# Inputs of the third and fourth superblock turned by VectorE and transfers through DRAM in place of TensorE

## The chip, the core and the metric

The kernel runs on one core of a Trainium2 chip. A core has engines with a queue of instructions each, worked off in order: TensorE (PE; matmuls, and the loading of their stationary operand, PEld), VectorE (DVE), ScalarE (ACT), GpSimd (POOL), and SyncE (SP), which here only issues transfers (DMAs). They meet at semaphores. Sixteen DMA engines move data between DRAM and the on-chip memory SBUF, whose 128 partitions are the first axis of every tile. TensorE writes to PSUM, a smaller memory of eight banks. The metric is the device time of one execution in microseconds (us).

## The reference

One transformer block with modulated normalization. `x` is 2048 rows of 512; `F` is 1376; all is 32-bit.

```python
mod = (silu(c) @ w_mod).reshape(1, 6, 1, 512)          # sa, ca, ga, sb, cb, gb
h = layernorm(x) * (1 + ca) + sa
x = x + ga * irfft2(rfft2(h) * (w_r + 1j * w_i))       # over rows and columns
h = layernorm(x) * (1 + cb) + sb
a = mish(h @ w1 + b1)                                  # 512 -> 1376
x = x + gb * (a @ w2)                                  # 1376 -> 512
```

## The kernel before

The first part (to about 90 us) does the spectral filter; its last phase, `p3_col` and `p3_row`, brings each of the 16 row tiles of `x` (128 rows each, kept in SBUF as `x[:, n, :]`) up to date. Then comes the second half, the two dense layers, which are interleaved with that last phase.

The two layers work on 8 blocks `b` of 256 rows, that is of two row tiles; two blocks are a superblock `i` (0 to 3, four row tiles `4i` to `4i + 3`). The hidden axis has six tiles `t`: five of 256 columns, and a single one, `t = 0`, of 96. Every 32-bit product is made of three terms: an operand is split into a high part, rounded by a ScalarE cast, and the rest, a VectorE subtraction (`split`, L848 to L850). Most tiles use a Strassen-like scheme with seven block products in place of eight. The right operands of the first layer are eight slots per superblock, four blocks of the transposed input (`B11`, `B12`, `B21`, `B22`) and four sums of them (`T1` to `T4`).

The steps on the way of an input are these.

- `norm_one(n)` (L207): ScalarE writes the normalized row tile `n` to a buffer of tag `h`, of which there are two.
- `next_in` (for the first superblock `first_in`) has two parts. `transpose_in` (L768) turns four pieces of 128x128 by TensorE into one PSUM bank of tag `D`; `scale_in` (L776) has ScalarE scale and shift them, two instructions of 128x256, into a buffer of tag `t` or `y`. Each superblock has four such steps, so 16 transposes.
- `sum_in` (L787) and `split_in` (L793, L794) make the eight slots.
- `up` (L914; `up_single`, L963, for the tile of 96) is one block product of the first layer, six matmuls into PSUM; its weights come from a ring of eight buffers `wr`, filled from DRAM by `fetch_w1` on SP's queue (L722), which waits there until the buffer is free. `evict` and `mish_odd` apply bias and activation. `sums` and `halves` (L987, L849, L850) prepare the activations, and `down` (L1017; L1013 for the tile of 96; `last_down` at the end, L1029 and L1032) is a piece of the second layer, three matmuls.
- `gather`, `chain` and `residual` bring a block's results together; a GpSimd DMA adds them to `x` in place (L1069), and `store` writes two row tiles of `x` to the output (L1078, SP's queue). After `store` the row tiles of that block are not read again. `load_last` later loads second-layer weights into `x[:, 0:2]`, `x[:, 2:4]`, `x[:, 4:6]` and `x[:, 6]` and multiplies them by the gate (L869).

The order of all this is written out by hand. `plan.at(key, fn, ...)` enters each step with a key; the steps are sorted by key and numbered, and the list `ORDER` then gives the sequence in which the numbers are issued. This sequence is the program order of every engine's queue. Below, "step 442" is the place in that sequence, counted from 0. A step's instructions go to the queues of their engines; between engines only data dependencies hold.

Of the kernel before, what the change touches and what calls it, by code (L numbers as in the profile page):

```python
# [7 lines left out]
F32 = mybir.dt.float32  # L8
F32R = mybir.dt.float32r
AF = mybir.ActivationFunctionType  # L10
ALU = mybir.AluOpType

P = 128
# [18 lines left out]
POOL_LOW = range(1, 15, 2)  # L32

ORDER = (
# [43 lines left out]
)  # L78


# [1 line left out]
def tile_spectral_block(ctx: ExitStack, tc: tile.TileContext, x_d, w1_d, b1_d, w2_d,  # L82
                        c_d, xt_d, wm_d, wq_d, wz_d, kr_d, km_d, kc_d, ki_d, kf_d, kv_d, kw_d, kp_d, out_d):
    nc = tc.nc
# [8 lines left out]
    dram = ctx.enter_context(tc.tile_pool(name="dram", bufs=1, space=bass.MemoryType.DRAM))  # L93
# [20 lines left out]
    def buf(tag, dt=F32):  # L114
        return work.tile([P, 512], dt, name="buf", tag=tag)

    def plain(t):
        return t.bitcast(F32)

    x = base.tile([P, N2, D], F32, name="x")  # L120
# [9 lines left out]
    cols = base.tile([P, 2, 2, 4], F32, name="cols")  # L130
# [82 lines left out]
    st = {}  # L213
# [483 lines left out]
    odd = [pm.tile([P, 512], F32, name=f"odd{i}") for i in range(4)]  # L697
    slots = {b: pm.tile([P, 2, 2, 256], F32R, name=f"h{b}") for b in ("B11", "B21")}
    wsum = pm.tile([P, 512], F32, name="wsum")
    ring, raws, src, temps, stage = {}, {}, {}, {}, {}  # L700

    def flat2(t):
        return t.rearrange("p a b -> p (a b)")
# [67 lines left out]
    def scale_in(b, g, dst):  # L771
        raws[b] = dst
        ps = st.pop("pt2")
        for e in range(2):
            k = 2 * g + e
            nc.scalar.activation(dst[:, 256 * e:256 * e + 256], ps[:, 256 * e:256 * e + 256],  # L776
                                 AF.Identity, bias=cols[:, 1, 0, k:k + 1], scale=cols[:, 1, 1, k:k + 1])

    def part(b, i):
        return slots[b][:, i].rearrange("p k s -> p (k s)")  # L780

# [4 lines left out]
        raws[b] = raws[dst] if dst in raws else dst if dst is not None else buf("h")  # L786
        nc.vector.tensor_tensor(raws[b], p, q, op=op)  # L787

    def split_in(b):
        r = raws[b]  # L790
        if b not in slots:
            slots[b] = pm.tile([P, 2, 2, 256], F32R, name="h" + b, tag="h" + b)
        nc.scalar.copy(part(b, 0), r)  # L793
        nc.vector.tensor_tensor(part(b, 1), r, plain(part(b, 0)), op=ALU.subtract)  # L794

    def p3_col(n):
        d = dd[n // 8][:, n % 8]
# [307 lines left out]
    plan = Plan()  # L1105
# [90 lines left out]
    for k, (i, t, j) in enumerate(units):  # L1196
# [6 lines left out]
        if (i, t) in PLAIN:  # L1203
            f, e = int(j[0][1]) - 1, int(j[1][2]) - 1
# [11 lines left out]
    for b in range(NB):  # L1216
        for t in DOWN if b < NB - 1 else (1, 2, 3, 4, 5, 0):
# [14 lines left out]
            n = len(order(b, t))  # L1232
# [14 lines left out]

    for i in range(1, NB // 2):
        u = where[i, 1, 1] - 39
        for n, s in ((0, 14.5), (1, 15.5), (2, 19.5), (3, 20.5)):  # L1250
            plan.at(u + s, norm_one, 4 * i + n)
        for b, n, g, s in (("B11", 0, 0, 17), ("B21", 0, 1, 18), ("B12", 2, 0, 23), ("B22", 2, 1, 25)):
            plan.at(u + s + 0.3, next_in, b, 4 * i + n, g)
        split_at, sum_at = (((35.2, 36.2, 37.2, 38, 37.5, 38.7, 40, 40.5), (35.4, 38.2, 36.5, 39.2)) if i == 1 else
                            ((33.3, 33.8, 37.3, 38.3, 39.3, 40.3, 41.3, 42.3), (34.65, 35.15, 36.65, 38.15)))
        for b, s in zip(("B11", "B12", "B21", "T2", "T1", "T3", "T4", "B22"), split_at):
            plan.at(u + s, split_in, b)
        for (b, dst), s in zip((("T1", "B11"), ("T3", "B12"), ("T2", None), ("T4", "B21")), sum_at):
            plan.at(u + s, sum_in, b, dst)

# [184 lines left out]
```

## Time and profile before

| | |
|---|---|
| median of 3 runs | 375.84 us (375.76 to 377.65) |
| profiled execution, its own time | 375.52 us |
| its span, first to last instruction | 373.7 us |
| TensorE clock granted | 0.997 |
| TensorE busy | 366.8 us |
| VectorE busy | 304.8 us |
| ScalarE busy | 252.5 us |
| DMA | 81.59 MB, 218 GB/s mean |

In rows of groups, the columns are: line, engine, operation, output and inputs, shapes, count, then the busy time in us and the mean ns of one, then the engine's idle time ahead of them and what ended it. The busy time of overlapping instructions is counted once, so for pipelined matmuls it is less than count times mean. In rows of the timeline the first number is the start in us from the span's start, the second how long the merged piece lasted. In rows of DMA issues the last number is the median time from issue to landing.

### The profile page before, as it was taken

To read this page: it belongs to the slowest core of one execution; us is meant where nothing else is said; L and a number is where in the kernel's file an instruction comes from. 1 tells how busy PE (TensorE), PEld (TensorE's weight loads), DVE (VectorE), ACT (ScalarE), POOL (GpSimd) and SP (SyncE) were. 2 spreads that over 40 slices of the span, in tenths; PEclk is the share of its full clock that TensorE was granted. 3 is DMA by queue.
4 is the path that set the end of the run, shared out by engine and by line. 5 is a ranking of instruction groups with operands and counts; after the bars stand their busy time and mean duration, and the time that the engine had idled before them with its cause. 6 is when DMAs were issued, how large, how long until landed. Compare 5 with 4: busy or idle time off the path is not lost.

```text
span 373.7 us, 8193 instructions
## 1 busy us (share of the span) xinstructions
PE 366.8 (98%) x2916; PEld 351.8 (94%) x2916; DVE 304.8 (82%) x752; ACT 252.5 (68%) x553; POOL 65.0 (17%) x102
## 2 busy tenths in 40 slices
PE   8999999998999999999999999999999999999995
PEld 8999967777999999999999999999999999999994
DVE  2898968888989989999994589884569895788996
ACT  1798879996557869999666865665865653365750
POOL 0588738784000000000000100000000000000000
PEclk9999999999999999999999999999999999999998
DMA  7999998777734545677874696747855858695132
GB/s 244 366 323 352 344 375 302 227 211 262 240 132 148 202 142 184 220 256 242 290 232 151 181 233 214 209 140 192 261 147 194 209 185 283 158 332 137 45 58 112
DMA packets 44359, 81.59 MB, mean 218 GB/s; under 512 B 6784, under 2 KB 12000, under 8 KB 44064
## 3 DMA queue, kind: packets, MB, share of 16 engines
q1 hardware_dynamic: 41152, 70.46, 56.8%
q0 software_dynamic: 1008, 3.67, 6.0%
q10 hardware_dynamic: 2160, 6.95, 5.8%
q8 instruction: 23, 0.38, 0.4%
q14 instruction: 16, 0.13, 0.1%
HBM read 64.02 MB, written 13.37 MB: 207 GB/s over the span
## 4 chain that ended last, share of the span: by engine, by line
PE 91%; DVE 6%; issue 1%; ACT 0%; DVEq 0%; ACTq 0%
PE bank L914 28%; PE bank L1017 24%; PE bank L802 4%; PE bank L812 4%; PE bank L803 4%; PE bank L547 4%; PE bank L257 4%; PE bank L963 3%; PE bank L596 3%; PE bank L302 3%; PE bank L1013 3%; PE bank L527 2%; PE bank L768 2%; PE bank L313 1%; PE bank L304 1%; PE bank L303 1%
## 5 line engine op out<-in xcount | busy, mean ns | idle before, releaser
L1069 POOL DMA_DIRECT2D x<-modr x7 | 6.2, 889 | 263.6 <-ACT buf L776 121.4
L914 PE MATMUL bank<-hT,wr 128*128 128x256 f32 x360 | 51.2, 283 | 0.0
L914 PEld LDWEIGHTS bank<-hT,wr 128*128 128x128 f32 x360 | 46.7, 191 | 0.1
L914 PE MATMUL bank<-hB,wr 128*128 128x256 f32 x300 | 43.5, 284 | 0.0
L914 PEld LDWEIGHTS bank<-hB,wr 128*128 128x128 f32 x300 | 39.1, 191 | 0.0
L850 DVE TENSOR_TENSOR al<-buf,ah 128x512 fp32r<-128x512 f32 (+1 forms) x45 | 29.9, 668 | 7.9 <-ACT ah L849 7.6
L1017 PE MATMUL bank<-w2a,ah 128*128 128x256 f32 x161 | 35.1, 283 | 0.0
L1017 PE MATMUL bank<-w2b,ah 128*128 128x256 f32 x147 | 32.3, 283 | 0.0
L849 ACT CAST ah<-buf 128x512 fp32r<-128x512 f32 (+1 forms) x45 | 26.8, 604 | 7.0 <-PE bank L1017 5.8
L914 PE MATMUL bank<-hcr,wr 128*128 128x256 f32 x210 | 30.3, 284 | 0.0
L914 PEld LDWEIGHTS bank<-hcr,wr 128*128 128x128 f32 x210 | 27.3, 191 | 0.0
L1017 PEld LDWEIGHTS bank<-w2a,ah 128*128 128x128 f32 x161 | 26.8, 191 | 0.0
L802 PE MATMUL bank<-kc,d 128*128 128x128 f32 x128 | 24.8, 276 | 0.5 <-ACT d L440 0.5
L803 PE MATMUL bank<-kc,d 128*128 128x128 f32 x128 | 24.8, 275 | 0.0
L1017 PEld LDWEIGHTS bank<-w2b,ah 128*128 128x128 f32 x147 | 24.7, 192 | 0.0
L171 DVE BATCH_NORM_STATS2 st<-x 128x6 f32<-128x512 f32 x32 | 21.9, 686 | 0.2 <-DMA x<-in_A_x_dram 0.2
L1017 PE MATMUL bank<-w,ah 128*128 128x256 f32 x112 | 21.7, 286 | 0.0
L302 PE MATMUL bank<-buf,mring 128*128 128x512 f32 x48 | 20.6, 430 | 0.2 <-DVE buf L295 0.2
L802 PEld LDWEIGHTS bank<-kc,d 128*128 128x128 f32 x128 | 19.4, 192 | 0.7 <-ACT d L440 0.7
L803 PEld LDWEIGHTS bank<-kc,d 128*128 128x128 f32 x128 | 19.4, 192 | 0.0
L805 ACT COPY buf<-bank 128x512 f32<-128x512 f32 x16 | 9.4, 584 | 14.8 <-PE bank L803 14.6
L776 ACT ACTIVATE buf<-bank,cols 128x256 f32<-128x256 f32 x28 | 14.2, 565 | 6.7 <-PE bank L768 6.5
(292 smaller groups left out, 1102.8 us busy)
## 6 DMA issues: line engine op xcount, KB each, us to landing
wr<-w_S SPq DMA_DIRECT2D x60, 256.0 KB, 3.1
wr<-w_A SPq DMA_DIRECT2D x45, 256.0 KB, 3.1
w_S<-hT SPq DMA_DIRECT2D x20, 256.0 KB, 2.4
x<-in_A_x_dram SPq DMA_DIRECT2D x16, 256.0 KB, 4.9
xring<-in_x_t_dram SPq DMA_DIRECT2D x16, 256.0 KB, 5.1
w_A<-wr SPq DMA_DIRECT2D x15, 256.0 KB, 4.4
x<-modr POOLq DMA_DIRECT2D x7, 512.0 KB, 5.7
out_dram<-x SPq DMA_DIRECT2D x7, 512.0 KB, 4.5
```

Source lines behind the costliest of these rows:

```text
L171: nc.vector.bn_stats(t, x[:, n, :])
L257: nc.tensor.matmul(pgv[:, j], data(j), krs[:, j, :].rearrange("p (c q) -> p c q", c=2), start=True, stop=True)
L302: nc.tensor.matmul(pa, m[:, a, 0:128], g, start=(i == 0), stop=False)
L547: nc.tensor.matmul(pb[:, 0:w], kf[:, 0:128], z[:, 0:w], start=True, stop=True)
L776: nc.scalar.activation(dst[:, 256 * e:256 * e + 256], ps[:, 256 * e:256 * e + 256], AF.Identity, bias=cols[:, 1, 0, k:k + 1], scale=cols[: ...
L802: nc.tensor.matmul(o, dj[:, 0:128], kc[0][:, n, :], start=True, stop=False)
L803: nc.tensor.matmul(o, dj[:, 64:192], kc[1][:, n, :], start=False, stop=True)
L812: nc.tensor.matmul(px[:, j * P:(j + 1) * P], e[:, j * P:(j + 1) * P], kiv[:, j, :], start=True, stop=True)
L849: nc.scalar.copy(h, r)
L850: nc.vector.tensor_tensor(l, r, plain(h), op=ALU.subtract)
L914: nc.tensor.matmul(o, w[:, p, k, :], h[:, q, k, :], start=(first and n == 0), stop=(last and n == 5), skip_group_check=True)
L1017: nc.tensor.matmul(out_ps[b][n][:, 256 * half:256 * half + 256], a[p][:, e], w2[t][q][:, r], start=(t == 1 and half == 0 and i == 0), stop ...
```

## The change

For the third and fourth superblock (`i` of 2 and 3) `next_in` is replaced. The normalized row tile (`norm_one` as before) is turned by VectorE in square blocks of 32x32 (`turn_one`), two row tiles interleaved into a pair of row tiles of `x` that has been stored: rows 0 and 1 of `x` for both pairs of the third superblock, rows 2 and 3 and then 0 and 1 for those of the fourth. Four DMAs per pair, each from 32 partitions, write it to a DRAM tile so that the blocks come to their place (`turn_out`, 128 KB each, pieces of 1 KB). One DMA per slot reads 128 partitions of four pieces of 512 bytes back (`turn_in`, 256 KB). ScalarE then scales and shifts in place in SBUF (`scale_turned`, two instructions of 128x256 elements as before). The elements of a slot lie in another order than before, so `split_in` reads them through a rearranged view for these superblocks. The keys of these steps differ, and `ORDER` is another list, with 1170 numbers in place of 1150: all steps, also those the change doesn't otherwise touch, are dealt out anew.

```diff
 ORDER = (
-    "3 1 0 14 4 2 16 21 15 5 7 6 52 8 10 123 73 12 71 17 11 13 26 118 75 19 38 32 9 44 125 24 47 80 22-23 33 18 82 "
...
+    "3 1 0 2 5 16 21 52 6 15 7 32 8 10 4 12 17 13 11 14 73 24 19 38 47 26 9 22 75 62 23 71 27 20 69 118 18 25 29 "
...
+    def turning(row):
+        return x[:, row:row + 2, :].rearrange("p r d -> p (r d)").rearrange("p (c k n j) -> p c k n j", c=4, k=4, n=2)
+
+    def turn_one(n, row):
+        nc.vector.transpose(turning(row)[:, :, :, n % 2],
+                            st.pop(("h2", n)).rearrange("p (k c j) -> p c k j", k=4, c=4))
+
+    def turn_out(n, row):
+        turned[n] = t = dram.tile([P, 4, 256], F32, name=f"turned{n}")
+        for a in range(4):
+            nc.sync.dma_start(t[:, a].rearrange("(c i) s -> i c s", c=4),
+                              x[32 * a:32 * a + 32, row:row + 2, :].rearrange("i r d -> i (r d)")
+                              .rearrange("i (c s) -> i c s", c=4))
+
+    def turn_in(b, n, g):
+        raws[b] = dst = buf("ty"["B12 B22".find(b) >= 0])
+        nc.sync.dma_start(dst.rearrange("p (a s) -> p a s", a=4), turned[n][:, :, 128 * g:128 * g + 128])
+
+    def scale_turned(b, g):
+        for e in range(2):
+            k, o = 2 * g + e, raws[b].rearrange("p (a k s) -> p k a s", a=4, k=2)[:, e]
+            nc.scalar.activation(o, o, AF.Identity, bias=cols[:, 1, 0, k:k + 1], scale=cols[:, 1, 1, k:k + 1])
...
-    def split_in(b):
+    def split_in(b, i=0):
         r = raws[b]
...
-        nc.scalar.copy(part(b, 0), r)
-        nc.vector.tensor_tensor(part(b, 1), r, plain(part(b, 0)), op=ALU.subtract)
+        h, l = part(b, 0), part(b, 1)
+        if i > 1:
+            r = r.rearrange("p (a m j) -> p m a j", a=4, m=4)
+            h, l = (z.rearrange("p (m a j) -> p m a j", a=4, m=4) for z in (h, l))
+        nc.scalar.copy(h, r)
+        nc.vector.tensor_tensor(l, r, plain(h), op=ALU.subtract)
...
     for i in range(1, NB // 2):
         u = where[i, 1, 1] - 39
-        for n, s in ((0, 14.5), (1, 15.5), (2, 19.5), (3, 20.5)):
-            plan.at(u + s, norm_one, 4 * i + n)
-        for b, n, g, s in (("B11", 0, 0, 17), ("B21", 0, 1, 18), ("B12", 2, 0, 23), ("B22", 2, 1, 25)):
-            plan.at(u + s + 0.3, next_in, b, 4 * i + n, g)
+        if i == 1:
+            for n, s in ((0, 14.5), (1, 15.5), (2, 19.5), (3, 20.5)):
+                plan.at(u + s, norm_one, 4 * i + n)
+            for b, n, g, s in (("B11", 0, 0, 17), ("B21", 0, 1, 18), ("B12", 2, 0, 23), ("B22", 2, 1, 25)):
+                plan.at(u + s + 0.3, next_in, b, 4 * i + n, g)
+        else:
+            for n, row, s in ((0, 2 * i - 4, 19.5), (1, 2 * i - 3, 20.5), (2, 0, 22.5), (3, 1, 23.5)):
+                plan.at(u + s, norm_one, 4 * i + n)
+                plan.at(u + s + 0.3, turn_one, 4 * i + n, row - n % 2)
+                if n % 2:
+                    plan.at(u + s + 0.4, turn_out, 4 * i + n - 1, row - 1)
+            for b, n, g, s in (("B11", 0, 0, 25), ("B21", 0, 1, 25.5), ("B12", 2, 0, 28), ("B22", 2, 1, 28.5)):
+                plan.at(u + s, turn_in, b, 4 * i + n, g)
+                plan.at(u + s + 2, scale_turned, b, g)
...
         for b, s in zip(("B11", "B12", "B21", "T2", "T1", "T3", "T4", "B22"), split_at):
-            plan.at(u + s, split_in, b)
+            plan.at(u + s, split_in, b, i)
```

More of the change, by code (lines that the diff above doesn't have):

```diff
@@ L699, in tile_spectral_block @@
     wsum = pm.tile([P, 512], F32, name="wsum")
-    ring, raws, src, temps, stage = {}, {}, {}, {}, {}
+    ring, raws, src, temps, stage, turned = {}, {}, {}, {}, {}, {}
     def flat2(t):
```

85 rows, old and new, of the table ORDER are left out of this document.

## The prediction

> **What bounds the kernel now.** I read the page's first part, then the stretches of 10 us, then TensorE's timeline around the transposes, the groups, and last the DMA issues and the waits of SP's queue.
>
> ```profile
> span 373.7 us, 8193 instructions
> PE 366.8 (98%) x2916; PEld 351.8 (94%) x2916; DVE 304.8 (82%) x752; ACT 252.5 (68%) x553; POOL 65.0 (17%) x102
> PE 91%; DVE 6%; issue 1%; ACT 0%; DVEq 0%; ACTq 0%
> ```
>
> The profiled execution took 375.52 us (span 373.7 and 1.8 around it); the median of the runs is 375.84, so 0.3 is added at the end. TensorE holds 91% of the chain. Whether it is merely busy or truly without gaps is told by the stretches (columns: PE, PEld, DVE, ACT, POOL busy us of 10, clock, DMA share, GB/s):
>
> ```profile
> 200.00:210.00 10.00, 10.00 (x87) 10.00 (x86) 5.03 (x15) 7.10 (x14) 0.00 (x0) 1.00 0.55 163
> 210.00:220.00 10.00, 10.00 (x86) 10.00 (x86) 6.12 (x15) 7.08 (x15) 1.06 (x1) 1.00 0.73 181
> 250.00:260.00 10.00, 10.00 (x86) 10.00 (x85) 5.74 (x15) 4.95 (x13) 0.85 (x1) 1.00 0.65 166
> 260.00:270.00 10.00, 10.00 (x87) 10.00 (x86) 4.00 (x11) 8.24 (x18) 0.00 (x0) 1.00 0.86 261
> 350.00:360.00 10.00, 10.00 (x82) 9.64 (x81) 9.79 (x22) 5.86 (x12) 0.10 (x1) 1.00 0.01 2
> 360.00:370.00 10.00, 9.61 (x62) 8.61 (x61) 9.86 (x20) 3.78 (x8) 0.76 (x1) 1.00 0.41 105
> ```
>
> The first four hold the transposes to be removed: TensorE is full there at clock 1.00, while VectorE is at 40 to 70%. Only the last 20 us have VectorE full beside it. TensorE's timeline (start, us, what), and two rows of the chain:
>
> ```profile
> 200.32 0.88 PE L914 MATMUL bank<-hB,wr 128*128 128x256 f32 x6
> 201.04 1.03 PE L768 MATMUL bank<-ident,buf 128*128 128x128 f32 x8
> 201.83 0.36 PE L1017 MATMUL bank<-w2hi,ah 128*128 128x256 f32 x1
> 202.03 0.28 PE L1017 MATMUL bank<-w2a,ah 128*128 128x256 f32 x1
> 202.15 0.28 PE L1017 MATMUL bank<-w2hi,al 128*128 128x256 f32 x1
> 210.18 0.60 PE L768 MATMUL bank<-ident,buf 128*128 128x128 f32 x4
> 210.54 0.36 PE L1017 MATMUL bank<-w2c,ah 128*128 128x256 f32 x1
> 210.74 0.28 PE L1017 MATMUL bank<-w2b,ah 128*128 128x256 f32 x1
> 344.94 3.00 PE bank L914 x24
> ```
>
> The starts are the cost: a product (six matmuls) 0.72 us, one matmul 0.12, so a piece of the second layer (three) 0.36. Between the steps of 201.04 and of 344.94 the old list has 96 products (12 of them the single tile's), 198 pieces and 8 groups of four transposes: 69.1 + 71.3 + 3.5 = 143.9, and 344.94 - 201.04 = 143.90. So TensorE does not wait once there; its time is the sum of its work.
>
> **The change part by part.**
>
> *Transposes removed.* From 201.04 to 201.83 eight take 0.79 us, and the matmul behind them starts its successor after 0.20 in place of 0.12: 0.87 for eight. Four take 0.36 + 0.08 = 0.44. The third superblock has one group of eight and two of four, 0.87 + 0.44 + 0.44 = 1.75, the fourth four of four, 1.76: **-3.5 us**. The page's mean of 272 ns is a latency and would give 32 x 0.272 = 8.7, which the starts rule out.
>
> *ScalarE and VectorE.*
>
> ```profile
> L776 ACT ACTIVATE buf<-bank,cols 128x256 f32<-128x256 f32 x28 | 14.2, 565 | 6.7 <-PE bank L768 6.5
> L947 ACT ACTIVATE even<-even 128x256 f32<-128x256 f32 x12 | 4.9, 410 | 0.0
> L794 DVE TENSOR_TENSOR hT<-buf,hT 128x512 fp32r<-128x512 f32 x12 | 8.2, 686 | 2.1 <-ACT hT L793 2.1
> L438 DVE COPY d<-bank 128x256 f32<-128x256 f32 x5 | 2.1, 423 | 0.6 <-ACT d L440 0.6
> L1265 DVE TENSOR_TENSOR w2a<-modr,w2hi 128x1024 fp32r<-128x1024 f32 x1 | 1.2, 1216 | 0.0
> 206.49 0.42 DVE L943 TENSOR_TENSOR buf<-buf,bank 128x256 f32<-128x256 f32 x1 [4.66 <-PE bank L914]
> 347.98 0.42 DVE L950 TENSOR_TENSOR buf<-buf,bank 128x256 f32<-128x256 f32 x1 [0.47 <-PE bank L914]
> ```
>
> The 16 scalings stay; they read SBUF and not PSUM, so between 0.41 and 0.57 us each: at most 2.5 us less ScalarE work, worth nothing where ScalarE is not last. Eight new VectorE transposes of 128x512: no row shows one. Bounds: the copy of half the elements (0.42) and an operation over twice as many (1.22); I take 0.69, the row of equal size. 8 x 0.69 = 5.5 (3.4 to 9.7), 2.8 per superblock. They stand in stretches where VectorE has 3 to 6 us of 10 idle (it waited 4.66 us for TensorE at 206.49), so 0 on the path; without that cover each is paid in full. The splits of eight slots per superblock now read in runs of 32 elements: same element count, 0 to +0.1 each, hidden likewise. Banks D that the transposes took become free earlier: at most a gain, but TensorE has no wait to lose.
>
> *Transfers added.* Per superblock 8 writes of 128 KB and 4 reads of 256 KB, 2 MB: 4 MB on 81.6, at DMA shares of 0.55 to 0.86. Rows (last number, or min/median/max: us to landing; the three landing lines belong to the weight loads, the weight stores and the output stores):
>
> ```profile
> wr<-w_S SPq DMA_DIRECT2D x60, 256.0 KB, 3.1
> x<-in_A_x_dram SPq DMA_DIRECT2D x16, 256.0 KB, 4.9
> xring<-in_x_t_dram SPq DMA_DIRECT2D x16, 256.0 KB, 5.1
> b1n<-in_B_b_dram SPq DMA_DIRECT2D x1, 5.0 KB, 5.9
> L722 SPq DMA_DIRECT2D wr<-w_S x60: 319/320/825, 170.4 to 334.2; - x60
> DMA to landing us min/median/max: 2.4/3.1/7.1
> DMA to landing us min/median/max: 2.0/2.5/6.0
> DMA to landing us min/median/max: 2.6/4.5/6.3
> SPq L722 <- PE bank L914: 90.3, 78, 4.6
> ```
>
> 24 issues of 0.32 us are 7.7 us of SP's queue, which spends 90 us waiting for weight slots anyway. What matters is order. I count offsets: TensorE's work ahead of a step, so that 110.84 in the old list is 201.04 in the trace. In the new list the third superblock runs so. store(0), step 420, offset 110.8, lands after 4.5: 115.3; the first transposing step (442) stands at 115.2 and writes those rows, so VectorE waits about 0.2. Two at 0.69: 116.7. turn_out (457) stands at 118.4; four issues 1.3, landing 2.5: 122.2. The third transpose (472, offset 122.0) overwrites the rows being read: another 0.2 of VectorE. Queued behind it: the fourth (484) and `halves` of the next block (485), which TensorE needs only at 128.5 (507): six us of cover. Second turn_out (488, 125.2): +1.3 +2.5 = 129.0. turn_in for B12 waits for that on SP, not at its own 127.0; behind it there are the loads of four weight blocks, the first wanted at 137.5 (552). It lands 3.1 (512-byte runs as in xring: up to 5.1) later: 132.4 to 134.4. scale_turned (532) stands at 134.6 and has `halves` (540) behind it on ScalarE, wanted by TensorE at 136.8; two scalings and two casts are some 2.6 us, so data are needed by about 134.1. Margin +1.7 to -0.3. The fourth superblock: last turn_out (731) 174.2, arrival 181.3 to 183.3, wanted by ScalarE at 183.9: margin 2.6 or less. I charge **+0.3**, for the third superblock.
>
> [...] xring, with 512-byte pieces, took 5.1 us beside 4.9 for whole rows, so the trace says that such runs cost little, and the new transfers keep 1 KB and 512-byte runs.
>
> *The order.* All steps are dealt out anew. The work is the same, minus the transposes: offsets at the end 275.6 before, 272.1 after. Two places differ. The last norm sums come at offsets 103 to 112 in place of 50 to 57 (0.69 each, hidden). At the end `halves(7, 2, 0)` (1131) stands right ahead of the piece that needs it: up to 1 us of TensorE, but VectorE binds there. From its last wait at 347.98 to the end VectorE has the same list in both (only `split_w2` of tile 0 and one `plain_w2` change places), and its release, the product at 254.1 and not 257.6, comes 3.5 sooner. So the end moves with it: 0, bounds -0.3 to +1.
>
> **Sum.** 375.52 - 3.5 + 0.3 = 372.3 for the profiled execution; +0.3 for the median: **372.6 us**.
>
> **Rivals.** A: as forecast, 371.8 to 373.9.
>
> B: the legs are 0.6 to 1.4 us later than their medians. Four stand in a row in the third superblock (store, out, out, in); beyond the margin each us of each counts on TensorE. At 1 us each: 4 - 0.7 = 3.3 lost, 375.6: no difference. For it: the medians of 4.9 and 5.1 where queues were full. Against: DMA shares of 0.55 and 0.73 at the spot, and the fourth superblock's margin.
>
> C, slower: the same round trip blocks ScalarE at step 532 for long. It decides from 1.5 us per leg, when more than 5.4 is lost; at 1.75: 7 - 0.7 = 6.3, so 375.84 - 3.5 + 6.3 = **378.6**. At the largest landings (6.3, 6.0, 6.0, 7.1) data come at 141.9, 7.8 late, and 2.2 in the fourth: 382.3. Against: all four would have to be far above the median.
>
> D: runs are broken up as the bias load is (5 KB in 5.9 us): 128 KB are 26 times that, 150 us per leg, over 600 us in all. Pieces of 512 bytes speak against it. [...]
>
> E: TensorE gets no faster, since VectorE's end binds: 375.8. For it: 9.79 and 9.86 of 10 at the end. Against: VectorE waited for TensorE at 347.98, so that work is released by TensorE.
>
> **Chances.** A 0.60, B 0.16, C 0.17, D 0.01, E 0.06. Half a per cent, 1.9 us, is about what a measurement of this kernel can tell from no change: faster 0.60, same 0.22, slower 0.18. The range reaches from the lowest run less 3.5, with 0.5 of scatter (371.8), to C's value at 1.75 us per leg (378.6); it leaves out the upper half of C, D and a little below.
>
> **What would show it.** Right: no transposes in the third and fourth superblock, TensorE's stretches still at 10.00, its last matmul near 366; VectorE transposes of about 0.7 us; scalings at 0.41 to 0.57. Wrong: a wait of TensorE between 200 and 290 us that goes back over ScalarE or VectorE to the turned transfers; landings above 4 us; VectorE transposes over 1.2 us; or gaps of TensorE elsewhere, which would lie with the order.

## The result and the profile after

The changed kernel takes 372.36 us (median; 371.81 to 373.19), the kernel before 375.86: a ratio of 0.991, 95% interval 0.989 to 0.993. It is faster by 3.5 us. The profiled execution took 372.40 us, with a span of 370.5.

The head of the page of the changed kernel, and the engines' shares of its chain:

```profile
span 370.5 us, 8169 instructions
PE 363.6 (98%) x2884; PEld 348.6 (94%) x2884; DVE 309.9 (84%) x760; ACT 253.6 (68%) x553; POOL 64.8 (17%) x102
PE 84%; DVE 7%; ACT 5%; issue 2%; ACTq 1%; POOL 0%; DVEq 0%
```

TensorE has 32 instructions less and 3.2 us less busy time, VectorE eight more and 5.1 us more. (TensorE's share of the chain fell from 91% mainly because the chain takes another way back through the first 90 us: some 49 us of it lie on TensorE there in place of 75.) The stretches of 10 us of the changed kernel (columns as in the prediction):

```profile
200.00:210.00 10.00, 10.00 (x85) 10.00 (x85) 8.16 (x25) 7.91 (x15) 0.00 (x0) 1.00 0.68 216
210.00:220.00 10.00, 10.00 (x86) 10.00 (x85) 6.88 (x16) 6.95 (x14) 0.00 (x0) 1.00 0.90 279
250.00:260.00 10.00, 10.00 (x85) 10.00 (x85) 6.89 (x18) 5.39 (x12) 0.00 (x0) 1.00 0.60 168
260.00:270.00 10.00, 10.00 (x86) 10.00 (x85) 6.89 (x17) 6.41 (x14) 0.85 (x1) 1.00 1.03 297
```

TensorE is still full in each. VectorE rose from 5.03 to 8.16 and from 4.00 to 6.89 where it had room, and the DMA share from 0.73 to 0.90 and from 0.86 to 1.03.

To see where the 3.5 us lie I cut the execution in two at TensorE's first matmul of `p3_col` (out `bank`, in `kc,d`), which lies ahead of all inputs that are turned in the new way; ahead of it only the order of the steps differs. First the kernel before (TensorE's timeline, the last VectorE row), then the changed one (the same, and its row in the chain of the last products and VectorE's last wait):

```profile
90.02 0.49 PE L802 MATMUL bank<-kc,d 128*128 128x128 f32 x2 [0.46 <-ACT d L440]
368.94 1.34 DVE L1086 TENSOR_TENSOR x<-x,bank 128x512 f32<-128x512 f32 x3
```

```profile
90.40 0.49 PE L830 MATMUL bank<-kc,d 128*128 128x128 f32 x2 [0.46 <-ACT d L441]
341.82 3.00 PE bank L942 x24
344.86 0.42 DVE L978 TENSOR_TENSOR buf<-buf,bank 128x256 f32<-128x256 f32 x1 [0.47 <-PE bank L942]
365.83 1.34 DVE L1114 TENSOR_TENSOR x<-x,bank 128x512 f32<-128x512 f32 x3
```

Up to the last products, 344.94 - 90.02 = 254.92 us before and 341.82 - 90.40 = 251.42 after: 3.50 less, what was predicted for the transposes. From VectorE's last wait to its end it is 370.28 - 347.98 = 22.30 and 367.17 - 344.86 = 22.31: that tail moved as a whole. The first part is 0.38 longer; its end lies between 89.8 and 91.4 in the profiles of all kernels here, also among those with the same order, and why was not followed up. From here on the part behind it, "the rest", is compared: 280.26 us before, 276.77 after.

The groups of the new path (the transposes, and the scalings that now read SBUF), and its DMA issues (last number: median us to landing):

```profile
L784 DVE STREAM_TRANSPOSE x<-buf 128x512 f32<-128x512 f32 x8 | 5.4, 698 | 1.0 <-DMA turned<-x 0.7 <-ACT buf L208 0.3
L801 ACT ACTIVATE buf<-buf,cols 128x256 f32<-128x256 f32 x16 | 8.6, 596 | 1.2 <-DMA buf<-turned 1.2
```

```profile
wr<-w_S SPq DMA_DIRECT2D x60, 256.0 KB, 3.7
turned<-x SPq DMA_DIRECT2D x16, 128.0 KB, 2.9
buf<-turned SPq DMA_DIRECT2D x8, 256.0 KB, 3.5
```

A transpose takes 0.70 us; a scaling 0.60, more than the 0.57 of the old form that read PSUM; the two legs land in 2.9 and 3.5. ScalarE waited 1.2 us in all for turned data, and this is where (ScalarE's timeline):

```profile
222.88 2.07 ACT L801 ACTIVATE buf<-buf,cols 128x256 f32<-128x256 f32 x4
273.20 1.09 ACT L801 ACTIVATE buf<-buf,cols 128x256 f32<-128x256 f32 x2 [0.46 <-DMA buf<-turned]
275.43 1.09 ACT L801 ACTIVATE buf<-buf,cols 128x256 f32<-128x256 f32 x2 [0.77 <-DMA buf<-turned]
```

The third superblock's last scalings (222.88) waited for nothing; both waits are in the fourth, and no wait of TensorE follows them: behind the cut its timeline shows none above 0.2 us, before or after.

### The profile page after: what moved, and what is told of

Read it like the earlier page. It is cut to its first block, busy times and chain, and to the rows that moved or that the text cites. A ratio compares the mean times of both kernels' runs of the same rounds, so it can differ in the third digit from the quotient of the medians.

```text
span 370.5 us, 8169 instructions
## 1 busy us (share of the span) xinstructions
PE 363.6 (98%) x2884; PEld 348.6 (94%) x2884; DVE 309.9 (84%) x760; ACT 253.6 (68%) x553; POOL 64.8 (17%) x102
## 4 chain that ended last, share of the span: by engine, by line
PE 84%; DVE 7%; ACT 5%; issue 2%; ACTq 1%; POOL 0%; DVEq 0%
PE bank L942 28%; PE bank L1045 24%; PE bank L830 4%; PE bank L840 4%; PE bank L831 4%; PE bank L258 4%; PE bank L991 3%; PE bank L303 3%; PE bank L1041 3%; ACT buf L580 1%; PE bank L314 1%; PE bank L305 1%; PE bank L304 1%; ACT buf L579 1%; ACT d L441 1%
## 5 line engine op out<-in xcount | busy, mean ns | idle before, releaser
L597 PEld LDWEIGHTS bank<-kv,a_sb 128*128 128x128 f32 x126 | 15.4, 191 | 2.7 <-issue 2.2
```

What stands on the lines that cost most here:

```text
L597: nc.tensor.matmul(pd[:, i * P:(i + 1) * P], y[:, i * P:(i + 1) * P], kv[:, 0:128], start=True, stop=True)
```

## The experiments

Theory: the gain is TensorE's time for 32 transposes, paid in full, and all that took their place is hidden. Rivals: the new order or the freed banks brought it; or the new path costs something, and the margin of the round trip is thin. The results together ("rest" is from the one profiled execution, the last column is its difference from the changed kernel's 276.77; a profiled execution can lie well off the median of its kernel, as for VectorE's transposes twice, 375.78, the copy in the third, 375.46, and the second superblock turned too, 383.62):

| kernel | median us | ratio to before (95%) | rest us | more |
|---|---|---|---|---|
| changed kernel | 372.36 | 0.991 (0.989 to 0.993) | 276.77 | |
| transposes put back | 375.73 | 1.000 (0.999 to 1.001) | 280.13 | 3.36 |
| old order, no turn | 372.15 | 0.991 (0.990 to 0.993) | 276.73 | -0.04 |
| VectorE's transposes twice | 373.95 | 0.996 (0.995 to 0.997) | 279.48 | 2.71 |
| extra copy, every pair | 391.57 | 1.044 (1.042 to 1.046) | 296.37 | 19.60 |
| extra copy, third, second pair | 376.84 | 1.003 (1.001 to 1.005) | 280.39 | 3.62 |
| extra copy, fourth, second pair | 379.55 | 1.009 (1.006 to 1.011) | 283.51 | 6.74 |
| the same on POOL's queue | 385.35 | 1.026 (1.024 to 1.029) | 290.84 | 14.07 |
| the same on SP, scalings later | 375.83 | 1.000 (0.998 to 1.002) | 280.86 | 4.09 |
| second superblock turned too | 381.96 | 1.017 (1.015 to 1.019) | 288.19 | 11.42 |
| the same, scalings later | 387.41 | 1.030 (1.028 to 1.032) | 292.08 | 15.31 |

**The transposes put back.**

```diff
     def region(i, t, j):
         if j == 1:
             ups[i, t, "x"] = bank("A")
+            if i > 1 and t > 1:
+                for k in range(4):
+                    nc.tensor.transpose(ups[i, t, "x"][:, k * P:(k + 1) * P], ident, ident)
```

> The new kernel, with 32 TensorE transposes put back: eight groups of four, of the constant identity, into a bank A that the product behind them overwrites, spread over the third and fourth superblock. Nobody reads them; VectorE's transposes and the transfers stay. Theory (the gain is TensorE time that is paid in full, 0.44 us a group): 372.4 + 3.5 = 375.9 us, with TensorE's stretches still at 10.00 of 10. Rival (the gain came from the new order of steps, from free banks or from ScalarE reading SBUF): it stays within 1 us of 372.4.

375.73 us. In the profile 3.36 us for eight groups of four, 0.42 a group, where the starts had given 0.44. So these transposing matmuls, for which nobody waits, cost their place in TensorE's stream, and that covers all but 0.14 us of the gain.

**The old order without a turn.**

```diff
     def next_in(b, n, g):
-        transpose_in(n, g)
-        scale_in(b, g, buf("ty"["B12 B22".find(b) >= 0]))
+        if n < 8:
+            ...
+            return
+        raws[b] = dst = buf("ty"["B12 B22".find(b) >= 0])
+        for e in range(2):
+            k = 2 * g + e
+            nc.scalar.activation(dst[:, 256 * e:256 * e + 256], st["h2", n + e][:, 256 * g:256 * g + 256],
+                                 AF.Identity, bias=cols[:, 1, 0, k:k + 1], scale=cols[:, 1, 1, k:k + 1])
```

> The kernel before, in its old order, whose third and fourth superblock leave the turn out altogether: ScalarE scales the unturned tiles straight out of SBUF, and there are no TensorE transposes, no VectorE transposes and no transfers for it, so the matrices in these superblocks are the wrong ones. It shows what the removal is worth with nothing put in its place. Theory (all of the gain is the transposes' time, and VectorE's turns, the transfers and the new order cost or bring nothing on the path): 375.8 - 3.5 = 372.3 us, the new kernel's time within 0.4. Rival 1 (the new path costs hidden time on TensorE's path): 371.5 or less. Rival 2 (the new order brought part of the gain): 373.2 or more.

372.15 us, and a rest that differs from the changed kernel's by 0.04 us. With nothing in the transposes' place, in the old order, the kernel is no faster than the changed one. So the new path and the new order together cost or brought nothing; that neither hides behind the other is told by TensorE's timelines, which show no wait above 0.2 us behind the cut in either kernel. (The reverse, the new order with TensorE's turn, was not tried: the banks D that it needs are held there by the products.)

**VectorE's transposes twice.**

```diff
-        nc.vector.transpose(turning(row)[:, :, :, n % 2],
-                            st.pop(("h2", n)).rearrange("p (k c j) -> p c k j", k=4, c=4))
+        h = st.pop(("h2", n)).rearrange("p (k c j) -> p c k j", k=4, c=4)
+        for _ in range(2):
+            nc.vector.transpose(turning(row)[:, :, :, n % 2], h)
```

> The new kernel with each of VectorE's eight transposes made twice: 8 x 0.70 = 5.6 us more VectorE work, and each pair leaves 0.7 to 1.4 us later. Theory (VectorE has cover there, and the chain of turn, write and read has some slack): 372.4 us, at most 0.5 more. Rival (VectorE's time counts, or the chain to the scalings has none): up to 372.4 + 5.6 = 378.0, with waits of TensorE between 200 and 290 us.

373.95 us, 1.6 more: neither 0.5 nor 5.6. The profiled execution has the highest time of the eleven, with 2.71 more in the rest, so it shows where time goes and overstates how much. TensorE's two new waits (its timeline):

```profile
210.76 0.39 PE L1046 MATMUL bank<-w2b,al 128*128 128x256 f32 x1 [0.24 <-DVE al L879]
274.70 0.94 PE L943 MATMUL bank<-hT,wr 128*128 128x256 f32 x6 [1.54 <-DMA wr<-w_S]
```

VectorE's added time is mostly hidden: `al` at 210.76 stands behind the third superblock's first, doubled pair on VectorE and comes 0.24 us late, so the cover there is shorter than the 1.4 us that were added. In the fourth superblock the pair leaves later, SP's reads (270.52 in place of 268.48) wait longer, and a weight block queued behind them comes 1.5 us late. In the third, whose reads were issued 1.7 us later (220.48 for 218.07, less the 0.73 by which this execution started later), no wait of TensorE goes back to them. TensorE itself ran 0.6 late there (the piece at 210.76 starts 119.63 us behind the cut, the same one 119.02 in the changed kernel), so this shows a margin of at least 1.1.

**One more leg in the round trip.** First for all four pairs:

```diff
     def turn_in(b, n, g):
         raws[b] = dst = buf("ty"["B12 B22".find(b) >= 0])
+        if g == 0:
+            again = dram.tile([P, 4, 256], F32, name=f"again{n}")
+            nc.sync.dma_start(again, turned[n])
+            turned[n] = again
```

> The new kernel with one more leg in the round trip: each turned pair (512 KB) is copied once more from DRAM to DRAM before it is read, so that each of the four pairs comes some 3.5 to 5 us later, and SP's queue stands still for as long. Theory (the margin that was predicted, 1.7 us in the third superblock and 2.6 in the fourth, is real, and beyond it each us counts once a superblock): at 4 us a leg 2.3 + 1.4 = 3.7 us lost, 376.1 (373.5 to 378), with waits of TensorE that go back over ScalarE's casts and scalings to the read. Rival (the transfers have far more slack than was counted): 372.4 within 0.4, and no wait of TensorE there.

391.57 us: 19 lost, five times what was expected. A copy took 5.2 us in the median, not 4; the two of a superblock add up, since the second pair's writes stand behind the first copy on SP; and TensorE's stalls (8.45 us at 236.22 behind ScalarE's cast `ah`, 4.1 for a weight block) brought its clock down to 0.50 for a time, of which more below. Then for single pairs: `if g == 0 and n == 10` (third superblock, second pair) and `n == 14` (fourth).

> The new kernel with the extra copy in the third superblock's second pair alone (the leg whose margin was predicted as +1.7 to -0.3 us). In the run with a copy for every pair this copy held SP from 222.76 to 227.21, with its own issue some 5.1 us. With each VectorE transpose doubled, the same read came 2.4 us later without a wait of TensorE behind it. Theory now (the margin is larger than predicted, 2.4 to 3 us, since VectorE and SP run ahead of their places in the list): 5.1 less 2.4 to 3 = 2.1 to 2.7 us lost, 374.5 to 375.1, in one wait of TensorE that goes back over ScalarE's cast. Rival (the margin as predicted): 3.4 to 5.4 lost, 375.8 to 377.8.

376.84 us (median), 4.5 more, which is what the rival had (3.4 to 5.4). The profiled execution, 375.46, lies near the low end of the ten (375.39 to 378.98), and in it the rest grew by 3.62 us, also more than the 2.1 to 2.7 of the theory. Five of the ten had a mean clock of 0.993 to 0.995, which the profile of this one (0.997) can't account for. TensorE's waits in the profiled one:

```profile
228.00 0.39 PE L1049 MATMUL bank<-w2hi,ah 128*128 128x256 f32 x1 [0.99 <-ACT ah L881]
236.43 0.95 PE L946 MATMUL bank<-hB,wr 128*128 128x256 f32 x6 [0.99 <-DMA wr<-w_A]
274.57 0.95 PE L946 MATMUL bank<-hT,wr 128*128 128x256 f32 x6 [0.49 <-DMA wr<-w_S]
```

The reads came 3.9 us later (221.54 for 218.07 less the 0.41 by which this execution started earlier) and TensorE waited 2.0 there, once behind ScalarE and once for weights queued on SP behind the reads. The first is the path of the prediction's margin: the piece at 228.00 starts 138.01 us behind the cut, in the changed kernel 136.74, so 1.3 of the 3.9 us came through and the margin was some 2.6, above the predicted +1.7 to -0.3. Counted over both waits it is 1.9. The third row lies in the fourth superblock, which this edit does not touch: I come back to it.

> The new kernel with the extra copy in the fourth superblock's second pair alone: 5.2 us on SP's queue. Theory (what counts here is the weights queued behind the turned read on SP, not the turned data: with doubled VectorE transposes that read came 2.7 us late and TensorE waited 1.5 us for a weight block): 5.2 - 1.2 = 4.0 us lost, 376.4 (375 to 378), with a wait of TensorE for a weight block of w_S. Rival (the turned data's own margin of 2.6 us decides): 2.6 lost, 375.0, with a wait that goes back over ScalarE.

379.55 us; in the profile the rest grew by 6.74, and neither view had the price. The path is the rival's, over ScalarE; the theory's wait for a block of `w_S` is there, but with 0.37 us. TensorE's waits:

```profile
272.95 0.95 PE L946 MATMUL bank<-hT,wr 128*128 128x256 f32 x6 [0.37 <-DMA wr<-w_S]
280.40 0.98 PE L946 MATMUL bank<-hB,wr 128*128 128x256 f32 x6 [2.19 <-ACT odd L959]
282.77 1.65 PE L946 MATMUL bank<-hT,wr 128*128 128x256 f32 x6 [0.93 <-ACT buf L959]
```

These are 3.5 us, for reads 4.7 us late (276.86 for 271.18 and 0.99 of later start). The product at 280.40 waits for no turned data and no weights: it waits for ScalarE to evict a bank (`odd`, L959), and that instruction is queued behind a scaling that waits for its data (ScalarE's timeline):

```profile
278.90 1.09 ACT L805 ACTIVATE buf<-buf,cols 128x256 f32<-128x256 f32 x2 [5.16 <-DMA buf<-again]
279.90 0.45 ACT L959 ACTIVATE odd<-bank,b1n 128x256 f32<-128x256 f32 x1
```

The other 3 us are in stretches of 1 us (column behind POOL: granted clock):

```profile
280.00:281.00 1.00, 0.60 (x5) 0.60 (x6) 0.00 (x0) 0.35 (x1) 0.00 (x0) 1.00 1.10 365
281.00:282.00 1.00, 0.84 (x7) 0.54 (x5) 0.00 (x0) 0.73 (x2) 0.00 (x0) 0.74 0.96 358
282.00:283.00 1.00, 0.23 (x1) 0.23 (x2) 0.25 (x1) 1.00 (x3) 0.00 (x0) 0.50 1.04 402
287.00:288.00 1.00, 1.00 (x6) 1.00 (x6) 1.00 (x4) 0.00 (x0) 0.00 (x0) 0.50 0.75 221
288.00:289.00 1.00, 1.00 (x9) 1.00 (x8) 0.15 (x1) 0.00 (x0) 0.00 (x0) 0.85 0.06 18
```

From about 281.5 to 288.3 TensorE ran at half clock, with 5 to 7 matmuls touching a stretch of 1 us in place of 10 or 11, though it was at work again. Which of the two, ScalarE or SP, carries the wait was asked in two ways. The transfers of that superblock on another queue:

```diff
-            nc.sync.dma_start(t[:, a].rearrange("(c i) s -> i c s", c=4),
+            (nc.gpsimd if n >= 12 else nc.sync).dma_start(t[:, a].rearrange("(c i) s -> i c s", c=4),
...
-            nc.sync.dma_start(again, turned[n])
+            (nc.gpsimd if n >= 12 else nc.sync).dma_start(again, turned[n])
...
-        nc.sync.dma_start(dst.rearrange("p (a s) -> p a s", a=4), turned[n][:, :, 128 * g:128 * g + 128])
+        (nc.gpsimd if n >= 12 else nc.sync).dma_start(dst.rearrange("p (a s) -> p a s", a=4), turned[n][:, :, 128 * g:128 * g + 128])
```

> The same copy in the fourth superblock's second pair, but all transfers of that superblock's round trip (writes, copy, reads) go over POOL's queue, so that no weight load stands behind them. Theory (SP's queue carries the loss): at most 1 us lost, 372.4 to 373.4, with no wait for a weight block. Rival (the late data carry it): as with the copy on SP, 375 to 378, with waits that go back over ScalarE.

385.35 us. The theory had the loss gone with these transfers off SP's queue, and it grew; but this compares unlike things, since the data came later still. No wait for a weight block is left, and the wait behind ScalarE is four times as long (TensorE's timeline; then POOL's, the last read and what it waited for):

```profile
286.18 1.65 PE L946 MATMUL bank<-hB,wr 128*128 128x256 f32 x6 [9.14 <-ACT odd L959]
```

```profile
284.98 0.75 POOL L800 DMA_DIRECT2D buf<-again x1 [2.95 <-issue]
```

POOL's queue issued that read 9 us later than SP's did (284.98 for 276.86, with this execution starting 1.06 earlier). And the scalings later on ScalarE, with all transfers on SP:

```diff
-            for k in places:
-                fn, args = steps[k]
-                fn(*args)
+            seq = [steps[k] for k in places]
+            for k, (fn, args) in enumerate(seq):
+                if k == 798:
+                    scale_turned("B12", 0)
+                if k == 825:
+                    scale_turned("B22", 1)
+                if k not in (776, 781):
+                    fn(*args)
```

> The extra copy in the fourth superblock's second pair again, on SP's queue, but the scalings of that pair stand later on ScalarE, each right ahead of the first step that reads its result (split_in of B12, and the sum T2), about 6 and 11 us of TensorE's work behind their old places. The reads come as late as with the copy before. Theory (the loss comes from ScalarE, which waits at a scaling with evictions queued behind it that TensorE needs, not from the data's lateness and not from SP's queue): at most 1 us lost, 372.4 to 373.4, no wait of TensorE above 0.5 us between 270 and 290 us, and the granted clock stays at 1.00. Rival (late data or late weights): the loss stays at about 6.7 us, 378 to 380.

375.83 us. TensorE's longest wait behind the new places, and a later one:

```profile
279.43 0.95 PE L946 MATMUL bank<-hB,wr 128*128 128x256 f32 x6 [1.96 <-DMA wr<-w_A]
293.45 1.46 PE L946 MATMUL bank<-hT,wr 128*128 128x256 f32 x10 [0.23 <-DVE hT L826]
```

The wait behind ScalarE is gone and the clock of the profiled execution stays at 1.00, as the theory had it; but the next limit stands right behind: a weight block, queued on SP behind the copy, 2.0 us late. The loss falls from 6.7 to 4.1, not to 1. So both in-order queues carry it: first ScalarE's, then SP's. By the median the loss is 3.5 us in place of 7.2.

**The second superblock turned too.** If VectorE and SP have cover there, its four groups of transposes are another 1.75 us.

```diff
+    def spin_one(n):
+        st["s2", n] = o = buf("t")
+        nc.vector.transpose(o.rearrange("p (c k j) -> p c k j", c=4, k=4),
+                            st.pop(("h2", n)).rearrange("p (k c j) -> p c k j", k=4, c=4))
...
+    SPIN = ((187, spin_one, 4), (189, spin_one, 5), (190, spin_out, 4), (191, spin_out, 5), ...
+            (216, spin_in, "B11", 4, 0), (220, spin_in, "B21", 4, 1), (232, spin_in, "B12", 6, 0), (236, spin_in, "B22", 6, 1),
+            (234, scale_spun, "B11", 0), (240, scale_spun, "B21", 1), (256, scale_spun, "B12", 0), (262, scale_spun, "B22", 1))
```

> The new kernel with the second superblock's inputs turned the same way (its four groups of transposes on TensorE go, 4 x 0.44 = 1.75 us; four more VectorE transposes, 16 writes of 64 KB in 512-byte runs and 4 reads of 256 KB in 256-byte runs come in). Theory (what TensorE has to do is the time, wherever VectorE and SP have cover): 372.4 - 1.75 = 370.6 us. Rival (VectorE, 9.0 to 9.8 of 10 busy between 120 and 200 us, or SP's queue has no cover there): 372.4 or more, with waits of TensorE between 100 and 200 us.

381.96 us, 9.6 more than the changed kernel. TensorE's waits, and the scaling that stands ahead of the first of them on ScalarE:

```profile
171.58 1.65 PE L968 MATMUL bank<-hB,wr 128*128 128x256 f32 x6 [4.35 <-ACT kiv L1022]
175.76 0.58 PE L1071 MATMUL bank<-w2hi,ah 128*128 128x256 f32 x1 [2.53 <-ACT ah L903]
282.74 0.94 PE L968 MATMUL bank<-hT,wr 128*128 128x256 f32 x6 [1.52 <-DMA wr<-w_S]
```

```profile
169.25 1.09 ACT L824 ACTIVATE buf<-buf,cols 128x256 f32<-128x256 f32 x2 [5.93 <-DMA w_S<-hT]
```

VectorE made its transposes between 153 and 160 us and waited 0.25 us, so VectorE was not the limit. But the last write was issued at 165, the first read at 165.7, and ScalarE stood at the first scaling until 169.25. (The row names a weight store as what came last; the scaling reads the turned slot alone, whose read, at the 3.5 us of the changed kernel's median, lands at about the same time.) The same with the reads issued earlier and the scalings, two sums and a split put later (`(211, spin_in, "B11", 4, 0)`, `(266, scale_spun, "B11", 0)`, `(289, scale_spun, "B12", 0)`, `(290, sum_in, "T1", "B11")` and so on):

> The second superblock turned by VectorE too, as before, but its reads issued as soon as the pair is written, and its four scalings, the sums T1 and T2 and the split of B12 put later (6 to 15 us of TensorE's work behind the places of the version before), where the data should be there. Theory (what cost 11 us there was ScalarE waiting at the scalings): TensorE has no wait above 0.5 us between 100 and 200 us, 372.4 - 1.75 = 370.6 us. Rival (VectorE at 9.0 to 9.8 of 10 has no cover there, or SP's queue has none): 372.4 or more, with waits of TensorE that go back over VectorE or to weight blocks.

387.41 us, slower still. TensorE's longest wait, what ScalarE waited for ahead of it, and SP's issues that belong to it:

```profile
175.63 0.58 PE L1071 MATMUL bank<-w2hi,ah 128*128 128x256 f32 x1 [7.52 <-ACT ah L903]
```

```profile
174.76 0.40 ACT L726 CAST hT<-hT 128x256 fp32r<-128x256 f32 x1 [8.25 <-DMA w_S<-hT]
```

```profile
170.85 0.53 SPq L818 DMA_DIRECT2D buf<-turned  x1
171.50 0.58 SPq L735 DMA_DIRECT2D w_S<-hT  x1
```

ScalarE no longer stands at a scaling but at the cast of the next summed weight block, whose slot `hT` becomes free when the block is stored; that store stands on SP behind a turned read that waits for its writes. In this stretch SP also carries the weight stores, and in neither of the two placements of ScalarE's part did the queue have slack for the round trip. Neither version with less TensorE work came out faster than the changed kernel.

## Why the prediction was right

The forecast, 372.6 us with faster at 0.60, was right, and by its own mechanism; one term of the sum and one reading were not. Step by step:

- *TensorE does not wait, so its time is the sum of its work, and the transposes cost 0.44 us a group and not 0.272 a matmul.* Shown: -3.50 us in the trace, +3.36 with the transposes put back.
- *Eight VectorE transposes at 0.69, hidden.* 0.70 measured. That they were covered is shown by the old order without a turn; doubled, they cost 1.6 us, in the trace mostly by SP's queue (1.54 us of wait) and a little by VectorE itself (0.24).
- *ScalarE's scalings at 0.41 to 0.57 from SBUF.* Wrong: 0.60. Worth nothing on the path, as the prediction said, but the sign was wrong.
- *24 issues at 0.32 us on SP.* Too cheap: the writes took 0.44 each, the reads 0.53 (medians), 16 x 0.44 + 8 x 0.53 = 11.3 us in place of 7.7. Hidden.
- *The third superblock's chain, +0.3 us.* The term that was wrong. VectorE waited for the first pair's writes once, 0.7 us, and not twice 0.2; the last reads were issued by 219.3 and so, at 3.5 us, were there at about 222.8, a little ahead of the predicted 223.0 to 225.0 (132.4 to 134.4 behind 90.6: offset 0 lies at 90.2 before, and this execution is 0.38 later). ScalarE did not wait, and the charge was not paid. On ScalarE's path the margin was some 2.6 us where +1.7 to -0.3 had been worked out, and 1.9 with the weights behind the reads, to which no margin had been given.
- *The fourth superblock, margin 2.6 or less.* Here the waits of ScalarE were, 1.2 us. Three kernels whose fourth superblock is that of the changed kernel (the copy in the third, and both with the second turned) show TensorE waits there of 0.49, 1.52 and 0.82 us, which the profile of the changed kernel does not. All three were held up earlier, so this is no clean measurement, but the margin that TensorE has there can't be far from zero: I had charged the wrong superblock.
- *Runs of 512 bytes cost little, as xring shows.* The conclusion held for these transfers, the reading did not: the trace has the xring loads as one piece of 2048 bytes for each of 128 partitions (the page of the kernel before counts 5216 packets from 512 bytes to 2 KB in all, where the 16 loads alone would make 8192 of 512), so no row that the prediction shows has such runs. That they land in 3.5 us was a bet that came out well, and so was the low chance of D as far as it rested on that row.
- *The order, 0 (-0.3 to +1).* 0.04 us against the old order without a turn; the piece behind `halves(7, 2, 0)` does not wait.
- *VectorE's end follows TensorE's last products.* 22.30 and 22.31 us: rival E fell.

The profile came at 372.40 where 372.3 had been summed, but the +0.3 was not what made up the sum: without it 372.0 stands, and the first part of this execution happened to be 0.38 longer. Rivals B and C did not come about, but their mechanism is real: the copies show that beyond the margin lateness counts, first by ScalarE standing at a scaling, as C had it. C's price was too low, since it left out the clock: in the fourth superblock 3.5 us of waits cost 6.7. D fell: 128 KB in pieces of 1 KB landed in 2.9 us, 256 KB in pieces of 512 bytes in 3.5. Neither transposes single elements: VectorE turns the squares, and the transfers only place whole runs. What a transfer of single elements would take, no run here shows.

## What to carry to other kernels

Where TensorE's stretches are full at full clock and its timeline can be summed from starts, an instruction taken from it is worth its place in the stream, start to start (here 0.42 to 0.44 us for four transposes), and what replaces it is free as long as nobody in TensorE's chain waits (here to within 0.04 us). Look for what breaks that in the in-order queues and not in the transfer's duration alone: a step that waits for data holds up everything behind it on its engine (the scaling that waited 5.16 us ahead of a bank's eviction, for which TensorE waited 2.19) and on its DMA queue (the read that stood ahead of a weight block, for which TensorE waited 1.54). Put the consumer as late as its own reader allows, and count more than its length for a TensorE stall like those of 2.19 us and more: here 3.5 us of waits cost 6.7, with the clock at 0.50 behind them for 6.8 us.

## What had not been expected of the hardware

Stalls of TensorE halved its clock, with a delay and in portions of one length. In five kernels the granted clock was 0.50 for a time between the first matmul and the last: from 281.48 to 288.30 (6.8 us) with the copy in the fourth superblock, shown above; from 230.08 to 240.32 (10.2) and from 284.70 to 291.52 (6.8) with the copy in every pair; from 170.42 to 180.66 (10.2) with the second superblock turned; from 279.94 to 293.58 (13.6) with the transfers on POOL's queue; and from 171.0 to 181.2 (10.2) and 191.48 to 194.90 (3.4) with the second superblock turned and its scalings later. The edges are worked out from the mean clock of the 1 us stretches in which they lie. These are, for the copy in every pair, the second superblock turned, POOL's queue, and the last of the stretches:

```profile
230.00:231.00 1.00, 0.00 (x0) 0.00 (x0) 0.00 (x0) 0.31 (x1) 0.00 (x0) 0.54 1.03 208
240.00:241.00 1.00, 1.00 (x9) 1.00 (x9) 1.00 (x3) 1.00 (x3) 0.00 (x0) 0.84 0.39 68
284.00:285.00 1.00, 0.00 (x0) 0.00 (x0) 0.56 (x1) 0.30 (x1) 0.00 (x0) 0.85 0.95 242
291.00:292.00 1.00, 1.00 (x8) 1.00 (x8) 1.00 (x3) 0.00 (x0) 0.00 (x0) 0.74 0.89 258
```

```profile
170.00:171.00 1.00, 0.00 (x0) 0.00 (x0) 0.33 (x1) 1.00 (x4) 0.00 (x0) 0.71 1.15 342
180.00:181.00 1.00, 1.00 (x8) 1.00 (x8) 1.00 (x3) 1.00 (x3) 0.00 (x0) 0.67 0.20 76
```

```profile
279.00:280.00 1.00, 0.00 (x0) 0.00 (x0) 0.00 (x0) 0.00 (x0) 0.00 (x0) 0.97 0.15 55
293.00:294.00 1.00, 1.00 (x8) 1.00 (x8) 1.00 (x2) 0.54 (x2) 0.00 (x0) 0.71 0.67 244
```

```profile
191.00:192.00 1.00, 0.87 (x5) 0.87 (x6) 1.00 (x4) 1.00 (x4) 0.00 (x0) 0.74 0.20 76
194.00:195.00 1.00, 1.00 (x7) 1.00 (x6) 1.00 (x3) 0.62 (x1) 0.00 (x0) 0.55 0.77 277
```

A mean of 0.54 is 0.92 us at half clock, so the first begins at 230.08, and so on. The lengths, 3.42, 6.82, 10.24 and 13.64 us, are one to four times 3.41 us. With the copy in every pair the edges lie 0, 3, 16 and 18 times 3.41 us behind 230.08 (61.44 us for the 18), and with the second superblock's scalings later 0, 3, 6 and 7 times behind 171.00 (23.90 for the 7), so in these two the portions stand on a grid that goes on through work and stalls.

In each of the five, ahead of the first fall of the clock, TensorE had stood for a time: 2.19 us (from 278.21 to 280.40 with the copy in the fourth superblock; the clock fell at 281.48, 3.3 us after the stall's start and 1.1 after the work had begun again), 2.31 (from 227.77 to 230.08 with the copy in every pair), 2.89 (from 168.11 to 171.00 with the second superblock's scalings later), 2.90 (from 277.04 to 279.94 with POOL's queue) and 3.19 (from 167.23 to 170.42 with the second superblock turned); in the last four it still stood when the clock fell. A stall of 1.54 us had no such fall behind it (273.16 to 274.70, VectorE's transposes twice, clock 1.00 from 270 to 300 us), nor did one of 1.96 (277.47 to 279.43, scalings later with SP's queue, mean clock 1.00 in the profiled execution), though three of the ten executions of that kernel had a mean clock of 0.995. What decides between 1.96 and 2.19 us, these runs do not show.

A weight load's landing (`wr<-w_S`, median) rose from 3.1 to 3.7 us in the changed kernel and lay at 3.8 to 4.0 with VectorE's transposes twice, in the first four kernels with a copy and in the first with the second superblock turned. Whether the 4 MB of traffic does this or the place of the loads in the new order, no run here tells apart. And POOL's queue was the slower way for the same chain here: its last read came 9 us later than SP's.
